# Normalized rows transposed by the DMA crossbar instead of identity matmuls

One Trainium2 chip (trn2), one core. The metric is the device time of one execution in microseconds (us). Engines in the profile: PE is TensorE (PEld its weight loads), DVE is VectorE, ACT is ScalarE, POOL is GpSimd, SP is SyncE, which here only issues DMAs. A "q" after the engine's name is its sequencer. Line numbers are those of the kernel that ran, so from L109 on the changed kernel's lines stand three further down than those of before. PSUM is the memory that TensorE writes its sums to, in banks; a bank has to be emptied before it is used again. A DMA "lands" when all its data has arrived.

## The reference

One transformer block on 2048 tokens of width 1024, in bfloat16. A layer norm without weights, QKV, attention of each token to 8 earlier tokens two apart in 32 heads of width 32, an output projection with a residual, a second norm, and a feed-forward part g * u of width 3584 with a residual:

```python
x = A_x
h = x + _A_ref(_layernorm(x, axis=-1), A_wqkv, A_wo)
h2 = h + _B_ref(_layernorm(h, axis=-1), B_w_gate, B_w_up, B_w_down)
```

## The kernel before

Four chunks of 512 tokens. A matmul contracts over the partitions, so the normalized rows (tokens on partitions) have to be transposed before QKV and before the feed-forward part. One helper does both norms, 128 tokens at a time (32 calls in all):

```python
def layernorm_T(src, dstT, col):
    ...                                    # bn_stats, bn_aggr, rstd
    ln = lnp.tile([128, D], BF, tag="ln")  # pool of 4
    nc.vector.tensor_scalar(ln[:], src[:], mv[:, 0:1], rstd[:], ALU.subtract, ALU.mult)
    pt = pstp.tile([128, KO, 128], BF, tag="pt")
    for kk in range(KO):                   # KO = 8
        nc.tensor.transpose(pt[:, kk, :], ln[:, bass.ts(kk, 128)], ident[:])
    nc.scalar.copy(dstT[:, :, col:col + 128], pt[:])
```

Attention runs on VectorE in another layout. So q, k and v go to DRAM and come back; the writes are issued by SyncE, as all loads of x and weights are, in one in-order queue. Attention has the lowest priority and fills VectorE's spare time:

```python
# in qkv(c, lnT, blocks), after each output tile of 128 columns
sg = t1k.tile([128, TC], BF, tag="t1k")
nc.scalar.copy(sg[:], ps[:])
...
nc.sync.dma_start(qd[c]..., sg...)         # k and v: two DMAs each
# attention(c): qD, kD, vD <- DRAM by GpSimd's queue; 32 products of 128 x 4096 on VectorE; od <- oD; oT <- od
# wo_ln2(c, oT): projection, then
nc.vector.tensor_tensor(hs[t][:, bass.ts(hf, 512)], ps[:], hs[t][:, bass.ts(hf, 512)], ALU.add)
...
for t in range(4):
    layernorm_T(hs[t], lnT, t * 128)       # second norm
```

The order of the calls; each engine's order is fixed at build by a list scheduler that follows priorities:

```python
for c in range(NCH):
    qkv(c, lnTs[c], B0)                    # first half of QKV's columns
    if c + 1 < NCH:
        with prio(-10000 + 1000 * (c + 1)):
            lnTs[c + 1] = ln1(c + 1)       # first norm, ahead of nearly everything
    else:
        with prio(1000000):
            oT = attention(0)
        nxt = wo_ln2(0, oT)
    qkv(c, lnTs[c], B1)
for c in range(NCH):
    lnT2, hs = nxt
    hT = ffn1(c, lnT2)
    if c + 1 < NCH:
        with prio(1000000 + (c + 1) * 20000):
            oT = attention(c + 1)
        nxt = wo_ln2(c + 1, oT)
    ffn2(c, hT, hs)
```

## Time and profile before

| | before |
|---|---|
| median of 3 runs | 855.85 us (854.95 to 856.88) |
| TensorE busy, of a span of 853.2 us | 827.4 us (97%) |
| 256 transposes, in the groups by line | 21.3 us of TensorE, 15.7 us idle before them |
| VectorE | 465.1 us (55%), but without a break from 63 to 430 us |
| DMA engines, first 63 us | 0.95 of 16 engines |

The groups' busy times are not the price of the transposes, because they overlap.

### The profile page before, as it was taken

The page shows a single profiled execution, that of the slowest core. Times are in us where ns is not written, and L with a number is a line of the kernel's source. Part 1 is how long each engine was busy: PE and PEld are TensorE (multiplying, and loading weights), DVE is VectorE, ACT ScalarE, POOL GpSimd, SP SyncE. Part 2 cuts the span into 40 slices and gives each one's busy share as a digit, 9 for nine tenths or more (in the row PEclk, how much of TensorE's full clock was granted, in tenths as well). Part 3 has the DMA queues.
Part 4 walks back from the last instruction along what each step waited for, and adds up shares of the span by engine and source line. Part 5 has one row for each costly group of instructions (what it writes and reads, how often), then busy time and mean ns, then how long its engine had stood idle before and what let it go on. Part 6 is the DMA issues. An engine that isn't in the chain of part 4 may idle for free.

```text
span 853.2 us, 9977 instructions
## 1 busy us (share of the span) xinstructions
PE 827.4 (97%) x4000; PEld 383.4 (45%) x4000; DVE 465.1 (55%) x523; ACT 234.6 (27%) x421; POOL 29.9 (4%) x46
## 2 busy tenths in 40 slices
PE   5999999969999997999999999999999999999998
PEld 4544444434444443444444444444444444444443
DVE  6719999998999999999931421111116102111011
ACT  4744333305333312003333120133332003333200
POOL 1000000200020000100000010000000000000000
PEclk9999999989999999999999999999999999999999
DMA  9896646975676743956455465653625465353520
GB/s 311 247 262 167 173 99 176 233 265 148 173 240 210 250 157 132 284 160 214 154 191 177 138 179 178 216 185 111 195 93 170 141 217 172 106 191 118 170 82 25
DMA packets 166798, 151.65 MB, mean 178 GB/s; under 512 B 55008, under 2 KB 159456, under 8 KB 164704
## 3 DMA queue, kind: packets, MB, share of 16 engines
q1 hardware_dynamic: 162912, 128.73, 50.3%
q0 software_dynamic: 3840, 22.28, 7.9%
q8 instruction: 31, 0.51, 0.2%
q14 instruction: 15, 0.12, 0.0%
HBM read 129.17 MB, written 22.02 MB: 177 GB/s over the span
## 4 chain that ended last, share of the span: by engine, by line
PE 68%; DVE 24%; ACT 3%; issue 2%; DMA 2%; SPq 0%; DVEq 0%; ACTq 0%
PE pu L255 21%; PE pg L251 21%; PE acc L290 16%; DVE prod L177 5%; DVE pv L208 4%; PE accl L277 3%; DVE prod L178 3%; PE ps L144 2%; PE ps L234 2%; DVE oD L214 2%; DVE st L100 2%; ACT lnT L112 1%; DVE pv L213 1%; DVE ln L108 1%; DVE ht L236 1%
## 5 line engine op out<-in xcount | busy, mean ns | idle before, releaser
L251 PE MATMUL pg<-lnT,wg 128*128 128x512 bf16 x896 | 211.7, 379 | 0.0
L255 PE MATMUL pu<-lnT,wu 128*128 128x512 bf16 x896 | 211.7, 379 | 0.0
L290 PE MATMUL acc<-wd,gs 128*128 128x512 bf16 x784 | 172.8, 381 | 3.1 <-DVE ht L236 2.3
L261 DVE TENSOR_TENSOR gs<-gs,us 128x512 bf16<-128x512 bf16 x112 | 47.2, 422 | 209.6 <-ACT us L260 209.6
L144 PE MATMUL ps<-lnT,wq 128*128 128x512 bf16 x736 | 161.3, 380 | 0.0
L258 ACT CAST gs<-pg 128x512 bf16<-128x512 f32 x112 | 65.7, 587 | 255.7 <-PE pg L251 254.6
L251 PEld LDWEIGHTS <-wg 128*128 128x128 bf16 x896 | 87.7, 98 | 105.7
L255 PEld LDWEIGHTS <-wu 128*128 128x128 bf16 x896 | 87.7, 98 | 105.7
L290 PEld LDWEIGHTS <-gs 128*128 128x128 bf16 x784 | 76.4, 98 | 94.8 <-issue 5.1
L144 PEld LDWEIGHTS <-wq 128*128 128x128 bf16 x736 | 71.9, 98 | 85.0 <-issue 0.8
L260 ACT CAST us<-pu 128x512 bf16<-128x512 f32 x112 | 65.7, 587 | 123.6 <-PE pu L255 122.4
L177 DVE TENSOR_TENSOR prod<-qD,kD 128x4096 bf16<-128x4096 bf16 x32 | 72.6, 2285 | 18.1 <-DMA kD<-kd 18.0
L147 ACT CAST sg<-ps 128x512 bf16<-128x512 f32 x96 | 55.8, 588 | 84.2 <-PE ps L144 79.1
L293 DVE TENSOR_TENSOR ht<-acc,ht 128x512 bf16<-128x512 f32 x28 | 17.4, 683 | 108.8 <-PE acc L290 108.8
L208 DVE TENSOR_TENSOR pv<-vD,at 128x4096 bf16<-128x4096 bf16 x32 | 72.4, 2286 | 0.3
L234 PE MATMUL ps<-wt,oT 128*128 128x512 bf16 x256 | 57.9, 387 | 3.4 <-DVE ht L236 3.4
L234 PEld LDWEIGHTS <-oT 128*128 128x128 bf16 x256 | 25.4, 99 | 35.3 <-issue 6.2
L178 DVE TENSOR_TENSOR prod<-prod 128x4096 bf16<-128x4096 bf16 x16 | 36.6, 2290 | 0.4
L111 PE MATMUL pt<-ident,ln 128*128 128x128 bf16 x256 | 21.3, 237 | 15.7 <-DVE ln L108 13.0
L112 ACT COPY lnT<-pt 128x1024 bf16<-128x1024 bf16 x32 | 31.1, 1012 | 10.2 <-PE pt L111 9.0
L104 ACT ACTIVATE lnv<-mv,eps 128x1 f32<-128x1 f32 x32 | 9.3, 295 | 80.2 <-DVE mv L102 80.1
L111 PEld LDWEIGHTS <-ln 128*128 128x128 bf16 x256 | 17.4, 106 | 24.4 <-DVE ln L108 22.1
(50 smaller groups left out, 330.0 us busy)
## 6 DMA issues: line engine op xcount, KB each, us to landing
wg<-in_B_w_gate_dram SPq DMA_DIRECT2D x28, 1024.0 KB, 5.3
wu<-in_B_w_up_dram SPq DMA_DIRECT2D x28, 1024.0 KB, 6.8
wd<-in_B_w_down_dram SPq DMA_DIRECT2D x32, 896.0 KB, 4.9
wt<-in_A_wo_dram SPq DMA_DIRECT2D x8, 1024.0 KB, 7.7
wq<-in_A_wqkv_dram SPq DMA_DIRECT2D x6, 1024.0 KB, 7.8
kD<-kd POOLq DMA_DIRECT2D x4, 1152.0 KB, 7.8
vD<-vd POOLq DMA_DIRECT2D x4, 1152.0 KB, 5.8
xt<-in_A_x_dram SPq DMA_DIRECT2D x16, 256.0 KB, 4.2
```

Of the source, the lines that this page charges most:

```text
L144: nc.tensor.matmul(ps[:], lhsT=wt[:, ko, bass.ts(j, 128)], rhs=lnT[:, ko, :], start=(ko == 0), stop=(ko == KO - 1))
L147: nc.scalar.copy(sg[:], ps[:])
L177: nc.vector.tensor_tensor(prod[:, j], qD[:], kD[:, :, o:o + SUB], ALU.mult)
L178: nc.vector.tensor_tensor(prod[:, :, 0:16], prod[:, :, 0:16], prod[:, :, 16:32], ALU.add)
L208: nc.vector.tensor_tensor(pv[:, j], vD[:, :, o:o + SUB], at[:, w, None, :].to_broadcast((128, DH, SUB)), ALU.mult)
L234: nc.tensor.matmul(ps[:], lhsT=oT[:, kk, t, :], rhs=wt[:, kk, :], start=(kk == 0), stop=(kk == KO - 1))
L251: nc.tensor.matmul(pg[:], lhsT=wg[:, ko, bass.ts(j, 128)], rhs=lnT[:, ko, :], start=(ko == 0), stop=(ko == KO - 1))
L255: nc.tensor.matmul(pu[:], lhsT=wu[:, ko, bass.ts(j, 128)], rhs=lnT[:, ko, :], start=(ko == 0), stop=(ko == KO - 1))
L258: nc.scalar.copy(gs[:], pg[:])
L260: nc.scalar.copy(us[:], pu[:])
L261: nc.vector.tensor_tensor(gs[:], gs[:], us[:], ALU.mult)
L290: nc.tensor.matmul(acc[t][:], lhsT=hT[f][:, bass.ts(t, 128)], rhs=wd[:, j, :], start=(f == 0), stop=(f == NF - 1))
```

## The change

The intent: take the transposes and their PSUM copies off TensorE and ScalarE, and let a DMA write the row already transposed. Chunk 0's first norm, for which everything waits at the start, keeps the old way.

```diff
-    def layernorm_T(src, dstT, col):
+    def layernorm_T(src, dstT, col, xbar=True):
 ...
         nc.vector.tensor_scalar(ln[:], src[:], mv[:, 0:1], rstd[:], ALU.subtract, ALU.mult)
+        if xbar:
+            nc.sync.dma_start_transpose(dstT[:, :, col:col + 128], ln[:])
+            return
         pt = pstp.tile([128, KO, 128], BF, tag="pt")
 ...
-            layernorm_T(xt, lnT, t * 128)
+            layernorm_T(xt, lnT, t * 128, xbar=(c > 0))
```

## The prediction

> **What bounds the kernel now.** I read the page first (busy shares, groups, the chain that ended last), then the stretches by stage, then the timeline of TensorE around every group of transposes, then the timeline of the issuing queue in the first 70 us.
>
> ```profile
> PE 827.4 (97%) x4000; PEld 383.4 (45%) x4000; DVE 465.1 (55%) x523; ACT 234.6 (27%) x421; POOL 29.9 (4%) x46
> ...
> PE 68%; DVE 24%; ACT 3%; issue 2%; DMA 2%; SPq 0%; DVEq 0%; ACTq 0%
> ...
> L111 PE MATMUL pt<-ident,ln 128*128 128x128 bf16 x256 | 21.3, 237 | 15.7 <-DVE ln L108 13.0
> L112 ACT COPY lnT<-pt 128x1024 bf16<-128x1024 bf16 x32 | 31.1, 1012 | 10.2 <-PE pt L111 9.0
> ```
>
> TensorE is busy 97% of the span and has most of the chain, so what leaves TensorE's instruction stream is a candidate for real gain. L111 is the transposes that the change touches, eight for each 128 tokens, 32 such blocks. Their row also says that TensorE stood idle 15.7 us before them, 13.0 for the normalized row (ln). L112, 31 us of ScalarE, is hardly on the chain: ScalarE is busy 27%.
>
> ```profile
> 24.00:63.00 39.00, 38.75 (x214) 18.36 (x213) 16.47 (x32) 20.28 (x43) 1.88 (x3) 1.00 0.96 260
> 63.00:143.00 80.00, 80.00 (x383) 36.72 (x383) 77.61 (x52) 30.50 (x51) 5.22 (x8) 1.00 0.56 141
> 143.00:213.00 70.00, 63.31 (x302) 29.41 (x301) 67.16 (x66) 20.65 (x39) 5.98 (x8) 0.95 0.81 224
> ...
> 317.00:358.00 41.00, 35.54 (x179) 15.91 (x177) 40.79 (x42) 5.45 (x12) 4.61 (x6) 0.96 0.61 194
> ```
>
> The columns are the stretch, then busy us of PE, PEld, DVE, ACT and POOL, the granted clock, the DMA share and GB/s. Up to 63 us the DMA engines are nearly full (0.96). From 63 to about 430 us VectorE runs the local attention without a break. The two stretches in which TensorE loses time (6.7 and 5.5 us) are the two in which it meets this busy VectorE: the output projection and second norm of chunks 0 and 1. After 358 us TensorE is alone the bound.
>
> **What the Trainium skill says.** "TensorE: Matmul & The Clock Gate", Part 4 (PE-mode transpose), gives about 275 ns for a 128x128 transpose in a kernel and 390 in isolation. The trace's mean of 237 is near, but it is a latency: in a row the transposes start far closer (below), so multiplying the count by it overstates the cost. "VectorE: DVE Perf Modes", The three transpose paths, gives 1309 ns for a 128x128 transpose by the crossbar. "DMA: Bandwidth & Descriptors", Latency and other measured facts, has 261 GB/s for DMA transposes with a non-contiguous middle dimension; the same page's section on issuing engines says that all queues share the same 16 engines. No run here has shown a crossbar transpose yet. Nearest in the trace are 256 KB loads of x, 4.2 us from issue to landing. Estimate from those two pages: 256 KB take between 1 us (261 GB/s) and 10.5 us (eight times 1309 ns); I take 3 to 6 us to landing and about 1 us of the 16 engines.
>
> **What is removed.** 28 of the 32 blocks: 224 transposes and 28 ScalarE copies. The matmul stream runs at one 512-column matmul per 0.216 us (eight in 1.73 us on the chain). Against it, the second norm of chunk 2:
>
> ```profile
> 492.12 1.10 PE L111 MATMUL pt<-ident,ln 128*128 128x128 bf16 x16
> ...
> 493.06 0.81 PE L290 MATMUL acc<-wd,gs 128*128 128x512 bf16 x3
> ...
> 494.18 0.61 PE L111 MATMUL pt<-ident,ln 128*128 128x128 bf16 x8 [0.31 <-ACT lnT L112]
> ...
> 494.62 2.32 PE L290 MATMUL acc<-wd,gs 128*128 128x512 bf16 x10
> ```
>
> Two blocks occupy 492.12 to 493.06, 0.94 us, and one occupies 0.44. Before 494.18 the three matmuls cover 0.65 of 1.12 us, so 0.47 is a wait. I went through all groups so. Blocks, from their first transpose to the next matmul: 12 of the first norm of chunks 1 to 3, 5.45 us; four of chunk 0's second norm, 2.58 (two at half clock, 1.68); twelve of chunks 1 to 3's second norm, 5.52. Sum 13.55 us. Waits just before them: 1.41 in the first norms, and 4.06, 2.68, 0.72 and 0.71 in the four second norms. Sum 9.58. The longest:
>
> ```profile
> 190.80 1.89 PE L111 MATMUL pt<-ident,ln 128*128 128x128 bf16 x16 [3.90 <-DVE ln L108]
> ...
> 192.49 3.41 PE L144 MATMUL ps<-lnT,wq 128*128 128x512 bf16 x12
> ```
>
> Here TensorE waits for ln though QKV matmuls that need none stand behind it. Three of those then run at 0.43 instead of 0.216 us: 0.64 lost. Upper bound of the gain: 13.55 + 9.58 + 0.64 = 23.8 us, which is 832. ScalarE's 28.3 us of copies lie beside other work and count nothing.
>
> **What is added and moved.** 28 transposes of 256 KB on the queue that also issues the loads and the writes of q, k and v, in order. Each has to wait there for its ln, and holds up what stands behind. In the second norms this is harmless: chunk 3's tiles are ready at about 658 us and needed at 704.6; chunk 0's at about 200 plus 3 to 6, needed from 205 or so. In the first norms it isn't, as the first attention hangs on this queue:
>
> ```profile
> 33.90 5.81 SPq L150 DMA_DIRECT2D qd<-sg  x8
> ...
> 59.76 4.51 DVE prod L177 x2
> ...
> 143.85 0.55 POOL L215 DMA_DIRECT2D od<-oD  x1 [3.33 <-DVE oD L214]
> ...
> 151.27 3.55 POOL L218 DMA_DIRECT2D oT<-od  x4 [6.87 <-DMA od<-oD]
> ...
> 166.35 9.01 PE L234 MATMUL ps<-wt,oT 128*128 128x512 bf16 x41
> ```
>
> The copies of q are made from 20.7 us on, but the queue comes to them only at 33.9, held up by x loads that wait for VectorE. Then it issues one write per 0.5 us and catches up at about 47. The k writes end at 53.3, k comes back at 59.7, VectorE starts attention 0 at 59.76 after 18.0 us of idling, and ends it at 143.6. The last quarter of oT lands at 162.9 in the trace, and TensorE wants it at 166.35: 3.5 us of slack.
>
> With 5.45 + 1.41 = 6.86 us less before it, TensorE is there at 159.5, so even undelayed oT costs 3.4 us of new waiting: gain 20.4. And I expect delay: about ten transposes enter the queue ahead of the k writes, at 0.5 us each or more (a plain issue takes 0.43) 5 us or more; the last of them wait for ln tiles that VectorE makes until 41.7; and their data, at 1 us each, go through engines already full at 0.96. Less the little slack by which the queue had caught up, I take 8 us: oT at about 171, a wait of 11.4 and a gain of 23.8 - 11.4 = 12.4 us, 843.4.
>
> **Rivals.** (1) Nearly the full gain, 832 to 836: the compile-time order puts chunk 3's second half of QKV (96 matmuls, 20.7 us) ahead of the projection that waits, or the queue isn't delayed. For it: the work is there and independent. Against: before, all 96 stand behind the projection, and the order is fixed at build. (2) The crossbar is slow, some 10 us for each 256 KB: twelve in the first 60 us add up to 100 us of a full DMA stage, attention 0 starts tens of us late, and TensorE has only 20.7 us to fill: 865 to 885. The 1309 ns speak for it if eight don't overlap; the 261 GB/s and the size of the plain loads' times speak against. (3) VectorE takes the waits' place: the removed waits for ln at 190.8 and 331.8 come back as waits for PSUM that VectorE empties behind attention products (as at 357, 0.78 us). VectorE is busy 99% there; another 3 to 6 us lost, 844 to 849.
>
> **Range and chances.** I give the first rival and its neighbourhood 35% (about 835), the middle case with or without the third 48% (843 to 848), the slow crossbar 17% (855 and up). The point is 842 us, the range 829 to 862. Faster by over 2% means under 838.7: 0.37. Slower by over 2% means over 873: 0.10. Within: 0.53.
>
> **What would show it.** L111 down to 32 transposes and L112 to 4 copies; matmuls after 478 us in an unbroken 0.216 us beat, so that the second norms of chunks 2 and 3 give 2.6 us each (right), or new gaps there (wrong). The start of attention 0: near 60 is rival 1, 65 to 70 my middle case, over 80 rival 2. A wait of the projection for oT of 3 to 12 us. A landing time of the transposes of 3 to 6 us; at 10 or more, with a DMA share still above 0.9 after 63 us, rival 2. I am wrong altogether if other DMAs are made to stand still while a transpose runs, which nothing in this trace shows.

## The result

845.27 us, median of 4 runs (844.55 to 846.10), against 855.68 for before on the same chip: ratio 0.988, 95% interval 0.9863 to 0.9897. All runs were fast ones (none over 1.5% above the fastest of its kernel). Ratios here are the mean time of one kernel's fast runs over that of the other's of the same rounds, so not quite the ratio of the medians quoted.

The page of the changed kernel, and from its list of DMA issues the new row (its columns: tile, queue, kind, count, median us to landing):

```profile
PE 811.4 (96%) x3702; PEld 372.0 (44%) x3776; DVE 464.9 (55%) x523; ACT 208.0 (25%) x393; POOL 30.1 (4%) x46
...
PE 57%; DVE 15%; issue 4%; DMA 0%; ACT 0%; DVEq 0%; ACTq 0%
...
lnT<-ln SPq DMA_TRANSPOSE x28, 4.7
```

PEld has all 3776 weight loads and PE only 3702 matmuls: 2% of the matmul records are missing, one about every 10.8 us. They look like gaps of one matmul and are none; I left them out of all counts below.

The second norm of chunk 2, in the timeline of the changed kernel (start, us, engine, line):

```profile
483.78 2.97 PE L237 MATMUL ps<-wt,oT 128*128 128x512 bf16 x13
484.51 1.24 SPq L110 DMA_TRANSPOSE lnT<-ln  x1
486.58 5.78 PE L293 MATMUL acc<-wd,gs 128*128 128x512 bf16 x25
```

The 13 matmuls of the projection take 486.58 - 483.78 = 2.80 us, 0.215 each, and the next ones follow without a gap. Where three groups of transposes and their waits stood, nothing is left; the transpose shown holds the queue 1.24 us, and TensorE not at all (others hold the queue up to 5.3 us).

The start of attention 0 and of the projection of chunk 0, with the writes of q that lead to them:

```profile
44.51 6.53 SPq L153 DMA_DIRECT2D qd<-sg  x8
...
71.61 4.50 DVE L180 TENSOR_TENSOR prod<-qD,kD 128x4096 bf16<-128x4096 bf16 x2 [16.78 <-DMA kD<-kd]
...
164.67 3.54 POOL L221 DMA_DIRECT2D oT<-od  x4 [7.65 <-DMA od<-oD]
...
170.64 1.89 PE L237 MATMUL ps<-wt,oT 128*128 128x512 bf16 x4 [6.12 <-DMA oT<-od]
```

Each stands later than its fellow before: the writes 10.6 us (33.9), attention 11.85 (59.76), oT's issue 13.4 (151.27), the projection 4.29 (166.35). TensorE now waits 6.12 us for oT, where it didn't wait at all.

To see where the time went I took the start of the first matmul of each part from both traces:

| first matmul of | before | after | gained so far | gained in between |
|---|---|---|---|---|
| projection, chunk 0 | 166.35 | 170.64 | -4.29 | -4.29 |
| feed-forward, chunk 0 | 212.82 | 207.94 | 4.88 | 9.17 |
| feed-forward, chunk 1 | 381.61 | 376.08 | 5.53 | 0.65 |
| feed-forward, chunk 2 | 543.05 | 534.96 | 8.09 | 2.56 |
| feed-forward, chunk 3 | 704.49 | 693.84 | 10.65 | 2.56 |
| end of the span | 853.18 | 842.78 | 10.39 | -0.26 |

The first norms lost time instead of saving some; chunk 0's second norm gave more than its transposes; chunk 1's gave almost nothing; chunks 2 and 3 gave what they should. Why, is the matter of the experiments.

One more new wait, which I hadn't foreseen, 50 us before the projection:

```profile
116.20 1.06 ACT L195 ACTIVATE lg<-lg 128x1024 f32<-128x1024 f32 x1 [11.34 <-DVE lg L194]
...
117.78 0.59 PE L147 MATMUL ps<-lnT,wq 128*128 128x512 bf16 x2 [3.23 <-ACT sg L150]
```

ScalarE's order has attention 0's exponential in the middle of QKV's copies out of PSUM. VectorE comes to it late, so ScalarE stands still 11.34 us, PSUM fills, and TensorE waits 3.23 us; the seven matmuls after it run at 0.43 instead of 0.216 us, 1.5 us more.

### The profile page after: what moved, and what is told of

Its sections match the earlier page's. It is cut to its first block, busy times and chain, and to the rows that moved or that the text cites. A ratio compares the mean times of both kernels' runs of the same rounds, so it can differ in the third digit from the quotient of the medians.

```text
span 842.8 us, 9480 instructions
## 1 busy us (share of the span) xinstructions
PE 811.4 (96%) x3702; PEld 372.0 (44%) x3776; DVE 464.9 (55%) x523; ACT 208.0 (25%) x393; POOL 30.1 (4%) x46
## 3 DMA queue, kind: packets, MB, share of 16 engines
q1 hardware_dynamic: 192480, 136.08, 56.5%
## 4 chain that ended last, share of the span: by engine, by line
PE 57%; DVE 15%; issue 4%; DMA 0%; ACT 0%; DVEq 0%; ACTq 0%
PE pg L254 17%; PE pu L258 17%; PE acc L293 17%; DVE pv L211 3%; PE ps L237 3%; PE accl L280 3%; DVE prod L180 2%; DVE pv L216 1%; DVE gs L264 1%; DVE oD L217 1%; DVE prod L181 1%; DVE t L184 1%; DVE prod L182 1%; DVE ht L239 1%; DMA vd<-sg 0%
## 5 line engine op out<-in xcount | busy, mean ns | idle before, releaser
L150 ACT CAST sg<-ps 128x512 bf16<-128x512 f32 x96 | 54.9, 586 | 78.6 <-PE ps L147 69.2
L211 DVE TENSOR_TENSOR pv<-vD,at 128x4096 bf16<-128x4096 bf16 x32 | 72.4, 2287 | 0.3
L100 DVE BATCH_NORM_STATS2 st<-xt 128x6 f32<-128x512 bf16 x32 | 20.3, 667 | 19.5 <-DMA xt<-in_A_x_dram 19.5
L216 DVE TENSOR_TENSOR pv<-pv 128x4096 bf16<-128x4096 bf16 x12 | 27.4, 2287 | 0.2
L217 DVE TENSOR_TENSOR oD<-oD,pv 128x4096 bf16<-128x4096 bf16 x12 | 27.4, 2285 | 0.2
```

The costliest lines, as they stand in the source:

```text
L211: nc.vector.tensor_tensor(pv[:, j], vD[:, :, o:o + SUB], at[:, w, None, :].to_broadcast((128, DH, SUB)), ALU.mult)
```

## The experiments

Twelve kernels in three groups; each group ran on one chip beside the kernel before (7 runs: medians 856.70, 856.35, 856.02). An edit is given against the changed kernel unless it says otherwise.

| run | median us | ratio to before | attention 0 starts | first projection |
|---|---|---|---|---|
| changed kernel | 845.27 | 0.9880 | 71.6 | 170.6 |
| e1 second norms alone | 845.70 | 0.9869 | 59.4 | 166.0 |
| e2 first norms alone | 854.53 | 0.9971 | 72.4 | 171.7 |
| e3 plain copies | 845.07 | 0.9862 | 73.8 | 170.4 |
| e4 transposes from ScalarE | 859.02 | 1.0031 | 67.1 | 174.4 |
| e5 first norms late | 848.32 | 0.9904 | 58.9 | 176.1 |
| e6 the same, in before | 860.10 | 1.0044 | 61.2 | 167.4 |
| e7 ScalarE evictions | 842.46 | 0.9838 | 69.7 | 166.7 |
| e8 e1 with ScalarE evictions | 841.62 | 0.9828 | 59.3 | 165.6 |
| e9 writes from ScalarE | 858.16 | 1.0014 | 72.8 | 178.6 |
| e10 the same, in before | 855.39 | 0.9987 | 62.7 | 168.1 |
| e11 ScalarE evictions, in before | 857.19 | 1.0011 | 59.5 | 165.8 |
| e12 e7 and e9 together | 853.04 | 0.9964 | 69.2 | 175.3 |

### e1 and e2: one half of the change each

```diff
-            layernorm_T(xt, lnT, t * 128, xbar=(c > 0))
+            layernorm_T(xt, lnT, t * 128, xbar=False)          # e1
...
-            layernorm_T(hs[t], lnT, t * 128)
+            layernorm_T(hs[t], lnT, t * 128, xbar=False)       # e2
```

> Crossbar for the second norm alone; all first norms back on TensorE. Theory A (the second norms carry the whole gain; the first norms' transposes pay for themselves with a late attention 0): attention 0 starts near 60 us as before, the first projection near 166, the first feed-forward near 205.5 (7.3 us earlier than before), and the kernel takes about 842.5 us, so less than the changed kernel's 845.3. Rival B (the first norms carry the gain, 6.9 us of it): about 852 us.

> Crossbar for the first norms of chunks 1 to 3 alone; all second norms on TensorE. Theory A: attention 0 starts near 71.6 us, the first projection near 170.6 instead of 166.4, and the kernel takes 855 to 860 us, no better than before (855.7). Rival B: about 849 us.

e1 took 845.70 us: rival B (852) is out, and the first norms' half of the change is worth nothing beside the other half (0.9869 against 0.9880, the intervals overlap). e2 took 854.53, just under theory A's 855 to 860 and far from B's 849; alone, this half gives 0.3%. Up to the feed-forward of chunk 0 theory A's numbers held: attention 0 at 59.4 us, the projection at 165.99, the feed-forward at 205.12 (205.5 expected). But the whole came out 3.2 us slower than expected. It was lost in chunk 1's second norm, where e1 needed 377.89 - 205.12 = 172.8 us from one feed-forward to the next, against 168.8 before. That part of theory A was wrong, and led to e7 and e8.

### e3: plain copies in place of the transposes

```diff
-            nc.sync.dma_start_transpose(dstT[:, :, col:col + 128], ln[:])
+            nc.sync.dma_start(dstT[:, :, col:col + 128], ln[:].rearrange("p (k s) -> p k s", s=128))
```

> The 28 transposes replaced by plain copies of the same tiles with the same 256-byte rows on the same queue (result wrong on purpose). Theory A1 (it is the place in the queue, its waits and the bytes that make attention 0 late): attention 0 starts at 69 to 72 us, kernel 844 to 846. Rival A2 (it is the crossbar itself, its longer issue of 1.3 to 5 us against 0.4): attention 0 starts at 62 to 66 us, kernel 839 to 842.

The result is wrong, on purpose. 845.07 us, and attention 0 starts at 73.8 us: A1's time, and a start even later than its 69 to 72. So plain copies with the same 256-byte rows do as much harm. But the comparison isn't clean, because the scheduler did not keep the copies' place. It put chunk 3's four between the writes of k, where the changed kernel has them behind the last one. SyncE's timeline, first of e3, then of the changed kernel:

```profile
55.06 4.48 SPq L110 DMA_DIRECT2D lnT<-ln  x4
```

```profile
62.02 9.32 SPq L110 DMA_TRANSPOSE lnT<-ln  x4
```

In e3 this splits the writes of k by 6.6 us (53.5 to 60.1); without it attention would start at about 67 (an estimate, 73.8 - 6.6), between A1 and A2. The first write of q, which comes earlier, is issued 7.1 us later than before in e3 and 10.6 in the changed kernel. So most of the delay needs no crossbar, and that the crossbar adds nothing is not shown.

### e4: transposes from ScalarE's queue

```diff
-            nc.sync.dma_start_transpose(dstT[:, :, col:col + 128], ln[:])
+            nc.scalar.dma_start_transpose(dstT[:, :, col:col + 128], ln[:])
```

> All 28 transposes issued from ScalarE's queue instead of SyncE's. If the late attention comes from standing in one queue with the writes of q and k: attention 0 starts at 58 to 63 us and the kernel takes 837 to 842. If it comes from the data on the 16 engines: about 70 us and 845. Rival: ScalarE has to wait for ln in its own order and PSUM is emptied late, with new TensorE waits of some us in the first 60 us: 848 or more.

859.02 us; the rival came true, and stronger than I had it. Chunk 3's four transposes need the lnT buffer that chunk 0's QKV matmuls release (in the changed kernel the trace has the first of them freed by those at 62.8 us). They stand before QKV's copies in ScalarE's order (timeline of this run):

```profile
68.34 9.06 ACTq L110 DMA_TRANSPOSE lnT<-ln  x4
77.45 3.03 ACT L150 CAST sg<-ps 128x512 bf16<-128x512 f32 x6 [21.26 <-DVE t L185]
78.08 0.58 PE L147 MATMUL ps<-lnT,wq 128*128 128x512 bf16 x1 [12.16 <-ACT sg L150]
```

ScalarE copies nothing for 21.26 us, and TensorE stands 12.16 us until it is through. Attention 0 starts at 67.1 us, between the two theories, so the run doesn't part them. It does measure the transposes by themselves, as they have a queue of their own here (queue, packets, MB, share of the 16 engines over the span):

```profile
q1 hardware_dynamic: 162912, 128.73, 50.2%
...
q10 hardware_dynamic: 29568, 7.34, 5.0%
```

5.0% of 854.8 us are 42.7 us of all 16 engines for 28 transposes: 1.5 us for each 256 KB, in 1056 packets.

### e5 and e6: the first norms of chunks 2 and 3 later

```diff
-            with prio(-10000 + 1000 * (c + 1)):
+            with (prio(-10000 + 1000 * (c + 1)) if c == 0 else nullcontext()):
                 lnTs[c + 1] = ln1(c + 1)
```

> The changed kernel, but the first norms of chunks 2 and 3 no longer run ahead: their loads and transposes stand behind chunk 0's writes of q and k in the queue. If the place in the queue makes attention 0 late, attention 0 starts at 55 to 62 us instead of 71.6, the first projection at 160 to 164 instead of 170.6, and the kernel takes 835 to 840 us. If it is the DMA engines' load, or if the norms are now held up behind attention on VectorE, the time stays at 843 or more.

> The same move of the first norms in the kernel before, with TensorE's transposes: the control. If the move is worth something only because the crossbar's transposes stand in that queue: 853 to 858 us, no change from before. If the move helps by itself (x loads no longer ahead of the writes): below 852.

e5's attention 0 starts at 58.9 us, so taking those transposes away from this time takes the delay away (in the control e6, where the loads of x move as well but no crossbar is used, it starts at 61.2, so moving the loads alone doesn't bring it forward). Yet the kernel took 848.32 us. Its VectorE (timeline):

```profile
57.68 1.29 DVE L100 BATCH_NORM_STATS2 st<-xt 128x6 f32<-128x512 bf16 x2 [35.81 <-DMA xt<-in_A_x_dram]
58.88 2.28 DVE L180 TENSOR_TENSOR prod<-qD,kD 128x4096 bf16<-128x4096 bf16 x1
61.08 0.20 DVE L102 BATCH_NORM_AGGREGATE mv<-st 128x2 f32<-128x12 f32 x1
61.20 0.64 DVE L100 BATCH_NORM_STATS2 st<-xt 128x6 f32<-128x512 bf16 x1
61.88 0.55 DVE L108 TENSOR_SCALAR ln<-xt,mv,rstd 128x1024 bf16<-128x1024 bf16 x1
```

It idles 35.81 us before the attention, and then makes the eight norms between attention's products. A norm costs 2 x 0.667 + 0.198 + 0.544 = 2.08 us, so eight add 16.6; attention 0 lasts 100.9 us (58.88 to 159.74) instead of 83.8, and ends 4.3 us later than in the changed kernel. The early norms had been free because VectorE was waiting for k anyway. e6 shows that the move costs almost 4 us by itself (860.10), which the expectation missed (853 to 858), though the scheduler put only four of the eight norms into attention 0 there. Between e6 and e5 the crossbar saves 11.8 us, about what it saves between before and after.

### e7, e8 and e11: ScalarE takes the sums out of PSUM

```diff
-                nc.vector.tensor_tensor(hs[t][:, bass.ts(hf, 512)], ps[:], hs[t][:, bass.ts(hf, 512)], ALU.add)
+                ev = t1k.tile([128, 512], BF, tag="t1k", name="ev")
+                nc.scalar.copy(ev[:], ps[:])
+                nc.vector.tensor_tensor(hs[t][:, bass.ts(hf, 512)], ev[:], hs[t][:, bass.ts(hf, 512)], ALU.add)
...                                         # and the same for acc[t] in ffn2
```

> The changed kernel, with the sums of the output projection and of the second feed-forward matmul (but the last) taken from PSUM by ScalarE, and added by VectorE from there. If the saving of chunk 1's second norm was eaten by waits for PSUM that VectorE empties behind attention products: the waits of 1 to 3 us between 314 and 353 us go, the second feed-forward (first matmul of chunk 1) starts at 371 to 373 instead of 376.1 us, kernel 840 to 842. If not: 844 to 847.

> The crossbar for the second norms alone, with the same ScalarE evictions. There the waits for PSUM were larger (4.6 us at 347 us, 3 us each at 176, 314 and 320), so the gain should be larger: 834 to 839 us against 845.7 without. If the waits were for something else: 844 to 847.

> ScalarE evictions in the kernel before: the control for the two runs with them. If they pay only where the crossbar has freed TensorE, 853 to 857; if they pay by themselves (before also waits for PSUM at 176, 320 and 324, some 8 us with the slow clock after it), 846 to 851.

Chunk 1's second norm, TensorE's timeline, first in the kernel before:

```profile
327.06 2.89 PE L290 MATMUL acc<-wd,gs 128*128 128x512 bf16 x6 [2.33 <-DVE ht L236]
331.83 1.08 PE L111 MATMUL pt<-ident,ln 128*128 128x128 bf16 x16 [1.88 <-DVE ln L108]
...
358.31 4.04 PE L290 MATMUL acc<-wd,gs 128*128 128x512 bf16 x18 [0.78 <-DVE ht L293]
```

then in e1:

```profile
316.97 3.61 PE L237 MATMUL ps<-wt,oT 128*128 128x512 bf16 x16 [2.53 <-DVE ht L239]
...
323.34 0.38 PE L293 MATMUL acc<-wd,gs 128*128 128x512 bf16 x1 [2.33 <-DVE ht L239]
...
352.30 25.75 PE L293 MATMUL acc<-wd,gs 128*128 128x512 bf16 x108 [4.25 <-DVE ht L296]
```

in the changed kernel:

```profile
321.54 0.38 PE L293 MATMUL acc<-wd,gs 128*128 128x512 bf16 x1 [1.35 <-DVE ht L239]
...
323.92 27.68 PE L293 MATMUL acc<-wd,gs 128*128 128x512 bf16 x112 [1.41 <-DVE ht L239]
352.99 7.28 PE L293 MATMUL acc<-wd,gs 128*128 128x512 bf16 x32 [1.38 <-DVE ht L296]
```

and in e7:

```profile
318.54 47.89 PE L295 MATMUL acc<-wd,gs 128*128 128x512 bf16 x217 [0.99 <-ACT ev L240]
```

In e1 the wait for ln is gone, and the one before the second half of the sums has grown from 0.78 to 4.25 us: TensorE came early to a PSUM bank that VectorE empties behind attention's products. (Another 1.9 us of e1's loss lies earlier, at 288 us: there TensorE waits for ScalarE, which has attention's exponential in its order.) With ScalarE as the one that empties, nothing of it is left: 217 matmuls in one piece, and the feed-forward of chunk 1 starts at 366.26 (376.08 in the changed kernel; 5.25 us of this difference were there at chunk 0's feed-forward already). Time is lost elsewhere, as ScalarE waits for attention's exponential and TensorE for ScalarE: in e7 3.3 us at 297 us, before this norm, and 3.8 at 394 us, behind it. The time was 842.46 us for e7 (expected 840 to 842, so just above) and 841.62 for e8 (expected 834 to 839, so the later loss was underrated). The edit makes VectorE lighter too: its add takes 415 ns from SBUF against 682 from PSUM, for 60 adds about 16 us in all; e11 shows that this alone gains nothing.

e11, the control, took 857.19 us: the same edit gains nothing in the kernel before. Its waits (engine, line, releaser, total us, times, longest), after those of before:

```profile
PE pt L111 <- DVE ln L108: 13.0, 6, 6.6
```

```profile
PE pt L111 <- DVE ln L108: 24.7, 8, 9.4
```

In e11 TensorE waits for no PSUM bank, and waits 11.7 us longer for ln. In one fixed order the two waits replace each other, whichever is removed. From chunk 0's feed-forward to chunk 1's it takes 168.8 us before, 172.8 in e1, 169.5 in e11, and 165.5 in e8: in this stretch only both together pay.

### e9, e10 and e12: the writes of q, k and v from ScalarE

```diff
-                    nc.sync.dma_start(qd[c][...], ...)      # and the two of k and v
+                    nc.scalar.dma_start(qd[c][...], ...)
```

> The changed kernel, with the writes of q, k and v issued by ScalarE, so that the transposes no longer stand ahead of them, and the norms keep their early place on VectorE. If the shared queue makes attention 0 late: it starts at 54 to 62 us and ends at 138 to 146, the first projection begins at 158 to 163 instead of 170.6, kernel 836 to 841. If the DMA engines' load makes it late: start near 70, 844 or more. Rival: ScalarE's issue time of about 0.45 us for each write makes it empty PSUM late, TensorE waits for it in the first 160 us, 848 or more.

> The same move of the writes in the kernel before: the control. Without transposes in the queue there is little to free: attention 0 starts at 52 to 58 us, kernel 852 to 858.

> Changed kernel with both: writes from ScalarE's queue and ScalarE evictions. If both causes are as told and add up: 832 to 837. If ScalarE becomes too busy: 842 or more.

e9 took 858.16 us. Attention 0 starts at 72.8 us though no transpose stands ahead of a write in any queue, and in the control e10 (855.39 us as expected) it starts at 62.7 (expected 52 to 58). The 10.1 us between them are nearly the 11.85 between before and after. So the delay doesn't need the shared queue, which the prediction had put first; my expectation fell. What stays is the load on the DMA engines. e9's queue of transposes shows it (timeline):

```profile
35.65 1.24 SPq L110 DMA_TRANSPOSE lnT<-ln  x1
38.03 14.37 SPq L110 DMA_TRANSPOSE lnT<-ln  x3
```

Alone an issue takes 1.24 us; here three hold the sequencer from 38.03 to 52.4, and a write of k issued at 35.1 lands at 42.5, one at 35.8 at 47.5. The first five writes of k take 7.4 to 11.8 us to land; in e10, without crossbar transposes, 1.9 to 5.6. Eight transposes come before the k writes: 8 x 1.5 us from e4 make 12 us of all engines, in a stage that was 0.95 full before them. That agrees with 11.85 and 10.1. It is an estimate: the share adds up the packets' times and reads up to 1.02 (e2, first 63 us). How much of it is bytes and how much the small packets, no run separates. Nor is the queue cleared for the changed kernel itself, where the first write of q is issued 10.6 us late behind the transposes: in e9 ScalarE's waits for its own writes come in the queue's place, and no run issues the writes from an idle engine. The rival of the expectation came true as well: TensorE waits 13.8 us for QKV's copies, because ScalarE now has to wait for its own writes. e12 (853.04) inherits that, and its 832 to 837 was wrong.

The fastest versions are e8 and e7, 1.7% and 1.6% under before; both beat the changed kernel, neither by 1% (each against before on its own chip).

## Why the prediction was right, and where it wasn't

**The direction and the size: right.** The middle case was 843.4, with the third rival 844 to 849, the point 842; measured 845.27, inside the range, and a change of less than 2%, the likeliest of the three outcomes. In part that is luck: the working has -4.5 us for the first norms and 7.3, 4.5, 2.6 and 2.6 for the second ones; measured were -4.3, 9.2, 0.65, 2.56 and 2.56. Three terms fit, and the second and third are off in opposite directions.

**What a block costs: right.** Chunks 2 and 3 were to give 2.6 us each, from blocks of 0.44 to 0.47 us and the waits before them; both gave 2.56. Reading the price from start to next start in the timeline held; count times the group's mean would have been 53 us, four times as much.

**The first norms lose what they save: right, but by luck, as errors cancel.** The prediction had the projection begin at about 171; it was 170.64. Its delay of attention 0, 8 us, was 11.85. Its slack of 3.5 us was read from the last quarter of oT, but the projection's first tile needs only the first, which landed at 155.9 us before (and at 170.59 after), so there were 10.5. Slack and delay were both too small. ("The k writes end at 53.3" is a slip too: the last lands at 52.7, and 53.36 is the issue of the load of k. The "about ten" transposes ahead of them were eight.) And the single wait of 11.4 us for oT became three: 3.2 us behind ScalarE's exponential, 1.5 of slow matmuls after it, 6.1 for oT.

**Why attention is late: two causes named, both sized too low, and their shares stay open.** The prediction counted queue time and engine time. e9 shows that the delay stays without the shared queue, e3 that most of it stays without the crossbar, e5 that it goes when the transposes go elsewhere. That the engines' load is the cause is what these leave, with e9's late landings; it is not shown by a run of its own. The queue's time was put at 0.5 us or more for each transpose; the trace has 1.24 or more. The engines' time was put at 1 us each; it measured 1.5.

**Chunk 0's second norm: mechanism right, size a little low.** It was to give 4.06 + 2.58 + 0.64 = 7.3 us and gave 9.17. Before, this stretch also has a wait of 2.8 us for VectorE, ended at 179.66 us, and seven slow matmuls behind it (1.5); after has neither, but twelve slow matmuls (2.6) behind the wait for oT. 7.3 + 2.8 + 1.5 - 2.6 = 9.0.

**Chunk 1's second norm: the term that failed.** 2.68 + 1.84 = 4.5 us were in the middle case's sum, and 0.65 came. At one matmul per 0.216 us the stretch from chunk 0's feed-forward to chunk 1's would take 158.9 us. Before, it takes 9.9 more: 1.8 for transposes, 2.7 waiting for ln, 4.6 waiting for PSUM that VectorE empties, 0.8 at half clock. In the changed kernel it takes 9.3 more: 6.4 waiting for PSUM and 2.9 at half clock. So the 4.5 us did go, and 3.9 came back in two ways. The first, 1.7 us, the third rival had said: waits for ln come back as waits for PSUM. e1 shows the new wait, e7 removes it, and e11 shows the reverse. It was a rival with the right mechanism and should have stood in the sum, as its sign was in the same line of the profile (VectorE 99% busy there). The second, 2.1 us, nobody had said: the granted clock, TensorE's share of full speed, stands at 0.5 for 6.8 us behind these waits instead of 3.4 (mean from 317 to 358 us: 0.92, before 0.96). e7 has no half clock in this stretch. (The rival's range was added up wrongly, too: 3 to 6 us on 843.4 are 846 to 849.)

**Landing in 3 to 6 us, no standstill of other DMAs: right in the median.** 4.7 us (4.5 for e3's plain copies), but up to 14.7 for one issued at 488.6 us, where nothing waits for it. Other DMAs went on: the loads of the gate weights land in 5.4 us, before in 5.3. Where the engines are full, e9's writes of k were held up, as told above.

## What to carry to other kernels

When an operation leaves the bounding engine, look at what stands next in that engine's fixed order: where another engine is full, the wait for its one product can turn into a wait for its next, as at chunk 1, where the gain came only when both went. A transfer moved to the DMA engines isn't free because the engine that issues it is idle: price it in time of all 16 engines, from a run in which it has a queue of its own, and set that against what is free in that stage. And work that looks early for no reason may be sitting in another wait's shadow, as the norms did before attention 0.

## What the Trainium skill lacked or had wrong

- "Advanced Engine Details and Errata", X-Bar Transpose (TRN2), says that transpose DMAs are as fast as regular ones and expects 350 to 400 GB/s. The first half agrees in landing for a copy of the same 256-byte rows (4.7 against 4.5 us, e3), but not in the engines' time: by the growth of SyncE's queue over before, which takes in what its other packets lost, 1.7 us for each transpose (56.5% of 842.8 us against 50.3% of 853.2) and 1.2 for each copy (55.0% of 842.1), an estimate. The rate was not reached: 256 KB took 1.5 us of all 16 engines (e4), 172 GB/s, among other traffic. "DMA: Bandwidth & Descriptors" with its 261 GB/s is nearer.
- "VectorE: DVE Perf Modes", The three transpose paths, has 1309 ns for one 128x128 block by the crossbar. It doesn't say how several blocks in one DMA add up: eight landed in 4.7 us (median), not in 10.5.
- No page gives, in us, how long the issue of a crossbar transpose of 256 KB within SBUF holds its queue on this chip: 1.24 us when nothing else held it (a plain DMA takes 0.43), and 14.4 us for three when the engines are full (e9).
